# A fused attention and two gated MLPs: two more groups of heads of the first batch score in float32, after transposes on the matrix engine

## The chip, the cores and the metric

The kernel runs on one core of a Trainium2 chip. A core has five engines that run side by side, each through its own list of instructions in a fixed order: TensorE (PE, with its weight loads as PEld), VectorE (DVE), ScalarE (ACT), GpSimd (POOL) and SyncE (SP), which here issues nearly all DMAs. They meet through semaphores. The metric is the device time of one execution in microseconds (us), the median of several.

## The reference

```python
q_n, k_n = rmsnorm(q, g_q), rmsnorm(k, g_k)          # q, k, v: 4 x 12 x 448 x 64, float32
attn = softmax(q_n @ k_n.T / sqrt(64))
x = (attn @ v).transpose(0, 2, 1, 3).reshape(4, 448, 768)
h = relu(x @ w_in)                                   # w_in: 768 x 1024
x = (h * sigmoid(conv3(h))) @ w_out                  # w_out: 1024 x 768
out = (sigmoid(conv5(x)) * (x @ w_val)) @ w_out2     # both 768 x 768
```

The float64 weights come in as pairs of 32-bit words and are made into float32 on the chip.

## The kernel before, in words

A program does not issue its instructions where they are written. It records them, each with a due time that the numbers `S_*`, `W_*`, `C_*` and so on set, in a `Plan`. The planner (`order`, `forward`) then runs a small model of the engines and of the DMA queues over the record and writes each engine's list. Some operations may go to one of two engines (`copy`: DVE or ACT; `sub` and `vg`: DVE or POOL), and the planner picks.

The work is four batches. Batch b has 21 attention units: 3 groups (`r`) of 4 heads, each group with 6 units of 128 query rows and one for the 64 rows left over. The MLPs of batch b run on PE while the attention of batch b+1 is worked on. The attention of batch 0 has no MLP beside it: there the weights are loaded, made into float32 and split in two float16 halves (tiles `w`, `wi`, `wo`).

Products are exact enough only if an operand is kept as a float16 pair, high and low, with three matmuls for one, or as float32. A group's `prep` loads q (`qin`) and k (`kin`, two pairs of heads), sums squares, takes the inverse roots (`ssq`, `half`, `root`, DVE), and scales k on POOL (`kin<-kin,gb`, `kin<-kin,root`). Then there are two ways to `qa` and `ka`, the operands of the scores with the head dimension on the partitions:

- not `flat`: `split_q` and `norm_k`/`low_k` write float16 pairs (`tq`; `tk`, whose second buffer in batch 0 lies in `act`), and `turn_q`, `turn_k` transpose them with a DMA (`DMA_TRANSPOSE qa<-tq`, `ka<-tk`). `qk` then issues three matmuls for each head.
- `flat`: q goes as it is and k as scaled float32 through PE transposes into PSUM (7 for q, 4 for each k, banks `psm`), a copy takes them to `qa` and `ka`, and `qk` issues one float32 matmul for each head.

Before, only group 0 of batch 0 is `flat` (`FLAT_0`); groups 1 and 2 are not, nor is any group of the other batches. In all of batch 0 the probabilities `p` are float32 and transposed by PE (`psm<-ident,p`, copied to `pt`); in batches 1 to 3 they are float16 pairs and transposed by DMA (`pt<-p`). After the scores (`pss`, two PSUM buffers) DVE takes the row maximum (TENSOR_REDUCE `pss<-pss`, one a unit), ACT the exponential. The three `psm` banks serve the transposes, the left-over units and the MLPs.

Of the kernel before, what the change touches and what calls it, by code (L numbers as in the profile page):

```python
# [15 lines left out]
ALU = mybir.AluOpType  # L16
# [9 lines left out]
class Plan:  # L26
# [10 lines left out]
    HOP = {"tensor": 0.2, "vector": 0.13, "scalar": 0.16, "gpsimd": 0.09}  # L37
    WINDOW = 23.016
    AHEAD = 50.91
    URGENT = 0.595  # L40
    TICK = 10.24 / 3
    ENTRY = 3060.0

# [193 lines left out]
    def order(self):  # L237
# [42 lines left out]
    def forward(self, first, users, port, shape):  # L280
        ops, nops = self.ops, len(self.ops)
        left = [len(o[1]) for o in ops]
        ready = [o[2] for o in ops]
        ends = [None] * nops
        waiting = {e: [] for e in Plan.ENGINES}
        free = dict.fromkeys(Plan.ENGINES, 1.05)
        free["sync"] = 0.58

        def enter(i):
            for e in ops[i][0]:  # L290
                waiting[e].append(i)
# [12 lines left out]
        def begin(i, e):
            t = max(free[e], hold[e], ready[i])
            at = held[other_of[e]] if port[i][e] else 0.0
            return at + self.KEEP if at > t else t

        while len(result) < nops:
            best = None  # L310
            for e in Plan.ENGINES:
                if waiting[e]:
                    t = min(begin(i, e) for i in waiting[e])
                    if best is None or t < best[0]:
                        best = (t, e)
            t, e = best
            pick = None
            turn = self.SWITCH if e == "tensor" else 0.0
            for _, i in sorted(
                (first[i] + (turn if turn and shape[i] != now_shape else 0.0), i) for i in waiting[e] if begin(i, e) <= t  # L320
            ):
                ways, lean = ops[i][0], ops[i][3]
                mine = t + ways[e][0][0] + lean.get(e, 0.0)
                other = min(
                    (max(free[x], t, held[other_of[x]] if port[i][x] else 0.0) + ways[x][0][0] + lean.get(x, 0.0) for x in ways if x != e),
                    default=1e9,
                )
                if mine <= other + 0.4:
                    pick = i
                    break  # L330
            if pick is None:
                hold[e] = t + 0.05
                continue
            i = pick
            hold[e] = 0.0
            (busy, lag, data), method, a, k = ops[i][0][e]
            if port[i][e]:
                t = max(free[e], ready[i], held[other_of[e]])
            for x in ops[i][0]:
                waiting[x].remove(i)  # L340
            if e == "tensor":
                busy, lag = self.clocked(t, busy, lag, counts), 0.0
                if now_shape not in (None, shape[i]):
                    busy += 0.1
                now_shape = shape[i]
            if method.startswith("dma"):
                t = max(since + 0.03 if e == "scalar" else t, ready[i], hwdge)
                hwdge = t + 0.45
                behind = max(dma - t - 1.28, 0.0)
                dma = t + 1.28 + behind + data  # L350
                end = t + lag + (0.8 if method == "dma_start_transpose" else 1.0) * behind
                busy += (0.35 if method == "dma_start_transpose" else 0.08) * behind
                busy = max(free[e] - t, busy)
            else:
                end = t + busy + lag
            if e == "scalar":
                since = t
            free[e] = t + busy
            ends[i] = end + (0.0 if method.startswith("dma") else self.HOP[e]), busy
            if port[i][e]:  # L360
                held[e] = t + busy - (0.06 if e == "vector" else 0.09)
            result.append((t, len(result), i, e))
            for u in users[i]:
# [14 lines left out]
def kernel(  # L378
# [15 lines left out]
    real, nc = tc.nc, Plan()  # L394
    B, H, S, D = q.shape
# [68 lines left out]
    def vg(lean, method, *a):  # L464

        nc.add([(e, method, a, {}) for e in ("vector", "gpsimd")], vector=lean)

    def sub(lean, out, x, y):
        vg(lean, "tensor_tensor", out, x, y, ALU.subtract)
# [26 lines left out]
    EARLY_W = 20  # L496
    S_TQ = 2.041
    S_DQ = 0.439
    S_K0 = 0.983
    S_K1 = 9.27  # L500
    S_DK = 1.448
    S_LQ = 3.68
    S_LK = -0.859
    S_G = -2.706
    DT0 = 2.39
    DT_1 = 5.2
    DT_2 = 5.592
    DT_3 = 7.99
    LAG = 2
    A_EXP = 0.719  # L510
    C_GATE = 1.87
    C_MUL = 2.053
    C_HI = 2.928
    C_LO = 3.1
    V_HI = 0.658
    A_HI = 0.853
    A_LO = 1.304
    A_OUT = 0.172
    E_PTR = 0.83
    E_AV = 2.135  # L520
    X_LAG = 1.873
    MPE = 96.0
# [4 lines left out]
    D_IN = 3.4  # L527
    L_TAP = -0.036
    LATE = 1
    LATE_F = 10  # L530
    FOLD_Q = 0
    FOLD_K = 0
    SIGN_IN = 1
# [5 lines left out]
    D_Y = 2.44  # L539
    KLEAD = 3.639  # L540
    QLEAD = 3.701
    VLEAD = 5.253
    STAT = 0.406
    KD_ = 1.21
    QD_ = 1.199
    W_IN = -74.315
    W_IN_STEP = 1.774
    W_OUT = -15.789
    W_OUT_STEP = 2.498
    W_VAL = 28.433  # L550
    W_VAL_STEP = 2.317
    W_2 = 87.193
    W_2_STEP = 3.986
    RS_AT = -0.54
    RS_STEP = 1.052
    BIG_IN = 1
    BIG_OUT = 1
    BIG_VAL = 0
    BIG_2 = 0
    OUT = (0, 0, 4, 4)  # L560
    FLAT_0 = 0.942
    FLAT_1 = 0.0
    FLAT_2 = 0.0
    WIDE_0 = 1
    WIDE_1 = 1
    WIDE_2 = 1


    L_SQ = 1.689
    L_LOAD = 3.419  # L570
    L_WHI = 1.553
    L_WLO = 0.899
    L_ROOT = 0.317
    L_QHI = 0.565
    L_QLO = 0.924
    L_GAIN = 1.803
    L_NORM = 4.34
    L_KHI = 1.236
    L_KLO = 0.76
    L_PLO = 0.459  # L580
    L_VM = -0.01
    L_VHI = 0.976
    L_VLO = 1.029
    L_PHI = 2.301
    L_PT = 4.563
    L_XHI = -0.2
# [33 lines left out]
    def close_bank(ps):  # L620
        in_use.pop(next(i for i, x in enumerate(in_use) if x is ps))
# [186 lines left out]
    def prep(b, r, t0, tq, dq, tk_, dk, ahead):  # L808
# [90 lines left out]
        def gain_k(i):  # L899
            x3 = of_k(i)[2]  # L900
            vg(lean(L_GAIN, S_LK), "tensor_tensor", x3, x3, gain_b, ALU.mult)

        def norm_k(i):
# [3 lines left out]
            if flat:  # L907
                by = rr[:KR, cols(i)].rearrange("p (h c) -> p h c", h=2).unsqueeze(3).to_broadcast([KR, 2, KC, D])
                to = o.rearrange("p a c d -> p (a c d)").bitcast(F32).rearrange("p (c h d) -> p h c d", c=KC, h=2)
                vg(lean(L_NORM, S_LK), "tensor_tensor", to, x, by, ALU.mult)  # L910
                return
            vg(lean(L_NORM, S_LK), "tensor_tensor", x3, x3, rr[:KR, cols(i)].unsqueeze(2).to_broadcast([KR, 2 * KC, D]), ALU.mult)
            copy(lean(L_KHI, S_LK), hi, x)

        def low_k(i):
            j, x, x3, o, hi, lo = of_k(i)
            assert holds["kin", i] == holds["tk", i if b == 0 else 0] == (b, j)
            if not flat:
                sub(lean(L_KLO, S_LK), lo, x, hi)

# [103 lines left out]
    def smax(u):  # L1024
        u.m = mx[u.n % 4]
        u.rq = root[(u.b * NPR // 2 + u.r) % 3]
        i0, i1 = u.parts[0][3](0), u.parts[0][3](1)
        m = u.ps[:, 0, S : S + 2]
        nc.vector.tensor_reduce(m, u.ps[:, :, 0:S], AX.X, ALU.max, negate=True)
        nc.vector.tensor_tensor(u.m, m, u.rq[:, i0 : i1 + 1 : i1 - i0], ALU.mult)  # L1030
        if u.out:
            vg(L_ROOT, "tensor_scalar", u.m, u.m, math.log(SP), None, ALU.add)

# [212 lines left out]
    for u in units:  # L1246
        t, d = T(u.n), T(u.n + 1) - T(u.n)
# [31 lines left out]
    def mlp(b, before):  # L1279
# [14 lines left out]
        def w_in_tile(f):  # L1294
            st = {}
# [27 lines left out]
                nc.scalar.activation(st["a"], st["a"], AF.Tanh, scale=0.5 / SX)  # L1323

            def mul():
                nc.vector.scalar_tensor_tensor(st["h"], st["a"], 1.0, st["h"], ALU.add, ALU.mult)

            def hi():
                g16[f] = take()
# [1 line left out]

            def lo():
                g = pairv(g16[f])
                nc.vector.tensor_tensor(g[:, 1], st["h"], g[:, 0], ALU.subtract)
                close_bank(st["ps"])

            group(st, [step(kk) for kk in range(KD)], D_IN)
            t = clock[0]
# [224 lines left out]
```

## Time and profile before

| | |
|---|---|
| median of 3 runs | 670.3 us (667.63 to 670.92) |
| the profiled execution's own time | 669.94 us, span 668.0 us |
| mean granted TensorE clock, share of full | 0.957 |
| busy PE / DVE / ACT / POOL | 584.2 / 517.2 / 420.1 / 224.3 us |

An engine's busy time is what its instructions cover; a share over the whole span says little where stretches differ, so the rows below go by stretch. Line numbers of instructions all read L374: that is the planner's `emit`, so instructions are told apart by their tiles.

### The profile page before, as it was taken

What the parts mean: (1) busy time and instruction counts of PE and PEld (TensorE: products, weight loads), DVE (VectorE), ACT (ScalarE), POOL (GpSimd) and SP (SyncE); (2) the same over time, 40 slices, a digit from 0 to 9 for tenths busy, and PEclk for the clock granted to TensorE, in tenths of its full rate; (3) what the DMA queues carried; (4) which work ended last, traced back from release to release, by engine and by line L of the source; (5) the groups of instructions that cost most, each with busy time, mean ns of one, the idle gap of its engine ahead of it and who ended that gap; (6) DMA issues with size and microseconds to landing.
All of it is one profiled execution on the core that took longest, in us unless ns stands there. A gap on an engine that the chain in (4) does not pass through costs nothing.

```text
span 668.0 us, 12681 instructions
## 1 busy us (share of the span) xinstructions
PE 584.2 (87%) x4753; PEld 329.7 (49%) x4753; DVE 517.2 (77%) x1061; ACT 420.1 (63%) x736; POOL 224.3 (34%) x241
## 2 busy tenths in 40 slices
PE   3866988876969789769897999999899999999997
PEld 1554766443434444335454555555455556445554
DVE  5798989999899998989659685659889663687720
ACT  4887899689868676978647465448765452342211
POOL 2344535254245225557634144405542210000000
PEclk9996999878998979989999899999999999999999
DMA  8887679979679859967978448556734735000001
GB/s 199 168 201 156 142 168 203 231 136 207 135 151 227 213 117 184 204 147 153 186 164 162 81 94 158 123 120 109 141 75 69 140 80 126 19 0 1 1 24 60
DMA packets 254894, 88.12 MB, mean 132 GB/s; under 512 B 240955, under 2 KB 250737, under 8 KB 254833
## 3 DMA queue, kind: packets, MB, share of 16 engines
q1 hardware_dynamic: 254833, 87.31, 63.5%
q8 instruction: 37, 0.61, 0.4%
q14 instruction: 24, 0.20, 0.1%
HBM read 38.66 MB, written 5.51 MB: 66 GB/s over the span
## 4 chain that ended last, share of the span: by engine, by line
PE 37%; DVE 26%; DMA 13%; ACT 13%; issue 5%; POOL 3%; SPq 2%; ACTq 0%; POOLq 0%; DVEq 0%
PE psm L374 29%; DVE act L374 7%; DMA pt<-p 6%; ACT p L374 5%; PE psx L374 4%; DVE pss L374 4%; DVE scr L374 4%; PE pss L374 3%; DVE w L374 3%; SPq L374 2%; ACT act L374 2%; DVE psm L374 2%; DMA ka<-tk 2%; DMA w<-in_moe_w_val_dram 2%; DVE p L374 1%
## 5 line engine op out<-in xcount | busy, mean ns | idle before, releaser
L374 PE MATMUL psm<-act,wi 128*128 128x448 f16 x576 | 125.0, 367 | 9.7 <-DVE act L374 8.1
L374 PE MATMUL psm<-act,wo 128*128 128x448 f16 x576 | 120.5, 360 | 0.2 <-DVE act L374 0.2
L374 DVE TENSOR_REDUCE pss<-pss 128x2 f32<-128x896 f32 x84 | 90.6, 1091 | 17.1 <-PE pss L374 15.2
L374 PEld LDWEIGHTS <-pt 128*128 128x128 f16 (+1 forms) x1512 | 66.8, 104 | 63.8 <-DMA pt<-p 43.5
L374 PE MATMUL psm<-w,act 128*128 128x384 f16 (+1 forms) x576 | 90.7, 326 | 2.2 <-ACT osb L374 1.9
L374 PE MATMUL psm<-act,wv 128*128 128x448 f16 x432 | 90.4, 357 | 1.8 <-DVE act L374 1.8
L374 ACT ACTIVATE p<-pss,mx,root 128x448 f32<-128x448 f32 x112 | 76.1, 723 | 22.7 <-DVE mx L374 13.0
L374 ACT ACTIVATE act<-psm 128x448 f16<-128x448 f32 (+4 forms) x90 | 47.8, 540 | 64.0 <-DVE psm L374 36.2
L374 PEld LDWEIGHTS <-wi 128*128 128x128 f16 x576 | 56.3, 101 | 64.1 <-issue 23.1
L374 PE MATMUL pss<-ka,qa 64*128 64x448 f16 (+3 forms) x560 | 71.1, 389 | 14.6 <-ACT p L374 6.1
L374 PEld LDWEIGHTS <-wo 128*128 128x128 f16 x576 | 55.1, 99 | 52.3 <-issue 9.0
L374 PE MATMUL psx<-vv,pt 128*128 128x65 f16 (+1 forms) x1116 | 79.8, 206 | 0.0
L374 PEld LDWEIGHTS <-act 128*128 128x128 f16 (+1 forms) x576 | 49.1, 101 | 33.7 <-issue 5.1
L374 POOL TENSOR_TENSOR p<-p,p 128x896 f16<-128x896 f32 x27 | 51.3, 1903 | 42.4 <-ACT p L374 36.2
L374 DVE SCALAR_TENSOR_TENSOR act<-psm,cw,act 128x444 f32<-128x444 f32 (+3 forms) x96 | 63.9, 676 | 0.7
L374 PEld LDWEIGHTS <-wv 128*128 128x128 f16 x432 | 40.7, 99 | 39.8 <-issue 6.8
L374 PE MATMUL psx<-vm,pt 128*128 128x130 f16 (+1 forms) x186 | 27.8, 244 | 31.5 <-DMA pt<-p 20.7
L374 DVE SCALAR_TENSOR_TENSOR scr<-psm,cw,scr 128x447 f32<-128x447 f32 x64 | 43.1, 677 | 2.7 <-ACT scr L374 2.1
L374 DVE SCALAR_TENSOR_TENSOR w<-w 128x768 uint32<-128x768 uint32 (+1 forms) x56 | 44.3, 796 | 0.0
L374 ACT ACTIVATE p<-p 128x896 f16<-128x896 f32 x42 | 40.0, 952 | 3.4 <-DMA pt<-p 3.0
L374 ACT ACTIVATE osb<-psm 128x384 f32<-128x384 f32 x28 | 13.6, 490 | 45.2 <-PE psm L374 34.3
L374 PEld LDWEIGHTS <-qa 64*128 64x128 f16 (+1 forms) x528 | 20.7, 99 | 41.4 <-issue 27.1
(123 smaller groups left out, 925.5 us busy)
## 6 DMA issues: line engine op xcount, KB each, us to landing
w<-in_moe_w_in_dram SPq DMA_DIRECT2D x8, 768.0 KB, 5.4
w<-in_moe_w_out_dram SPq DMA_DIRECT2D x8, 768.0 KB, 5.8
kin<-in_k_dram SPq DMA_DIRECT2D x24, 224.0 KB, 3.7
qin<-in_q_dram SPq DMA_DIRECT2D x36, 128.0 KB, 3.6
act<-in_moe_w_out_dram SPq DMA_DIRECT2D x12, 384.0 KB, 3.8
w<-in_moe_w_val_dram SPq DMA_DIRECT2D x12, 384.0 KB, 3.9
out_dram<-osb SPq DMA_DIRECT2D x24, 192.0 KB, 2.1
vst<-in_v_dram SPq DMA_DIRECT2D x18, 224.0 KB, 3.5
```

The source lines that it names most:

```text
L374: getattr(getattr(nc, e), method)(*a, **k)
```

## The change

`FLAT_1` and `FLAT_2` go from 0 to 1: groups 1 and 2 of batch 0 take the `flat` way too. The planner's model of DMA issues charges the issuing queue differently, and some 40 due times and leanings get new values. Two new switches, `MUL` and `LEAVE_IN`, are off and add no instruction.

```diff
-                end = t + lag + (0.8 if method == "dma_start_transpose" else 1.0) * behind
-                busy += (0.35 if method == "dma_start_transpose" else 0.08) * behind
+                end = t + lag + behind
+                busy += (0.15 if method == "dma_start" else 1.0 if data > 1.6 else 0.3) * behind
...
-    FLAT_0 = 0.942
-    FLAT_1 = 0.0
-    FLAT_2 = 0.0
+    FLAT_0 = 0.908
+    FLAT_1 = 1
+    FLAT_2 = 1
...
-    URGENT = 0.595
+    URGENT = 0.616
...
-    W_VAL = 28.433
-    W_VAL_STEP = 2.317
+    W_VAL = 26.105
+    W_VAL_STEP = 2.348
...
+    MUL = 0.0
+    LEAVE_IN = (0, 0, 0, 0)
```

Some 40 numbers more change in the same tables. What they and the planner make of it is seen in the lists of instructions, at three places.

On DVE, between the last row maximum of group 0 and the first of group 1 (`root_106` is group 1's inverse root, `kin`/`tk` and `kin`/`act` are the low halves of its two k). The end of that piece, before: 12 rows, the maximum itself comes 7 rows later.

```order
L374 TENSOR_REDUCE ssq_104<-act 128x14
L374 TENSOR_SCALAR rs_110<-psm_121 128x2
L374 RECIPROCAL rs_110<-rs_110 128x2
L374 TENSOR_TENSOR scr_95<-psm_121,rs_110 128x128
L374 TENSOR_TENSOR tk_86<-kin_83,tk_86 112x2x4x64
L374 TENSOR_SCALAR w_65<-w_65 128x768
L374 TENSOR_TENSOR act<-kin_84,act 112x2x4x64
L374 TENSOR_SCALAR rs_109<-psx_118 128x6
L374 TENSOR_TENSOR act<-psm_120,act 128x64
L374 RECIPROCAL rs_109<-rs_109 128x6
L374 CAST act<-psm_120 128x64
L374 TENSOR_TENSOR scr_96<-psx_118,rs_109 128x384
```

The changed program has, for the end of that piece, the maximum as the eighth row:

```order
L374 SCALAR_TENSOR_TENSOR root_106<-half_108,root_106 128x30
L374 SCALAR_TENSOR_TENSOR half_108<-root_106 128x30
L374 TENSOR_TENSOR half_108<-half_108,ssq_104 128x30
L374 SCALAR_TENSOR_TENSOR root_106<-half_108,root_106 128x30
L374 TENSOR_REDUCE ssq_104<-act 128x14
L374 CAST act<-psm_120 128x384
L374 TENSOR_TENSOR act<-psm_120,act 128x384
L374 TENSOR_REDUCE pss_117<-pss_117 128x2
L374 TENSOR_SCALAR rs_110<-psm_121 128x2
L374 TENSOR_REDUCE pss_116<-pss_116 128x2
```

Before, 25 rows stand between the two maxima, two of them k's low halves; now 14, and no split of k.

On PE, at the first scores of group 1 (`qa_69`). Before, they come straight behind batch 0's attention products and a transpose of the convolution weights (`act 128x24`); each score has a weight load of its own row.

```order
L374 MATMUL psx_118<-vm_75,pt_92 128x130
L374 MATMUL psx_118<-vv_71,pt_92 128x65 x6
L374 MATMUL psm_120<-ident,scr_95 128x128
L374 MATMUL psm_120<-ident,act 128x24
L374 LDWEIGHTS qa_69
L374 MATMUL pss_117<-ka_66,qa_69 128x448
L374 LDWEIGHTS qa_69
L374 MATMUL pss_117<-ka_66,qa_69 128x448
```

In the changed program the transposes of k (`ident,tk`, and `ident,act` for the second k) stand between the products, and a unit has four score matmuls:

```order
L374 MATMUL psm_120<-ident,tk_86 128x112 x4
L374 MATMUL psx_118<-vm_75,pt_92 128x130
L374 MATMUL psx_118<-vv_71,pt_92 128x65 x3
L374 MATMUL psm_120<-ident,scr_94 128x128 x3
L374 MATMUL pss_117<-ka_66,qa_69 128x448 x2
L374 MATMUL pss_116<-ka_66,qa_69 128x448 x2
L374 MATMUL psm_121<-vv_71,pt_93 64x65
L374 MATMUL psm_120<-ident,p_0_88 128x128 x3
L374 MATMUL psx_118<-vv_71,pt_92 128x65 x3
L374 MATMUL psm_120<-ident,act 128x112 x4
```

On SP, the queue of DMAs from group 1's first k on. Before:

```order
L374 DMA_TRANSPOSE ka_66<-tk_86 128x8x112
L374 DMA kin_83<-in_k_dram 112x8x64
L374 DMA kin_84<-in_k_dram 112x8x64
L374 DMA_TRANSPOSE ka_67<-act 128x8x112
L374 DMA w_65<-in_moe_w_in_dram 128x6x256
L374 DMA vv_71<-in_v_dram 128x7x64
L374 DMA w_65<-in_moe_w_in_dram 128x6x256 x2
L374 DMA_TRANSPOSE ka_66<-tk_86 128x8x112
L374 DMA kin_83<-in_k_dram 112x8x64
L374 DMA w_65<-in_moe_w_out_dram 128x1536
```

In the changed program the same loads stand without the transposes of groups 1 and 2; the first DMA transpose of the program is the one of batch 1 in the last row:

```order
L374 DMA kin_83<-in_k_dram 112x8x64
L374 DMA kin_84<-in_k_dram 112x8x64
L374 DMA vv_70<-in_v_dram 128x7x64
L374 DMA vv_71<-in_v_dram 128x7x64
L374 DMA w_65<-in_moe_w_in_dram 128x6x256 x2
L374 DMA qin_85<-in_q_dram 128x4x64
L374 DMA qin_85<-in_q_dram 64x2x64 x2
L374 DMA qin_85<-in_q_dram 128x4x64 x2
L374 DMA kin_83<-in_k_dram 112x8x64
L374 DMA kin_84<-in_k_dram 112x8x64
L374 DMA_TRANSPOSE qa_69<-tq_87 128x14x128
```

Over the whole program the changed lists have 6 DMA transposes fewer (2 of q, 4 of k), 30 PE transposes more (14 of q, 16 of k), 8 copies from PSUM more on ACT, 1 score matmul for each 3 in two groups, on DVE 3 float16 casts and 1 low half of q and 3 low halves of k fewer, on POOL 1 low half of q fewer, and 3 of the 8 low halves of `wi` that POOL did are now on DVE.

## Rows read from the trace of the kernel before

**Rows 1.** The page: busy time of each engine, share of the span.
```profile
PE 584.2 (87%) x4753; PEld 329.7 (49%) x4753; DVE 517.2 (77%) x1061; ACT 420.1 (63%) x736; POOL 224.3 (34%) x241
```

**Rows 2.** Busy time by stretch; columns: PE, PEld, DVE, ACT, POOL, clock, DMA share.
```profile
16.50:40.70 24.20, 20.95 (x140) 14.35 (x136) 20.82 (x46) 20.79 (x38) 9.96 (x7) 1.00 0.76 171
40.70:52.90 12.20, 6.73 (x71) 5.36 (x71) 11.26 (x26) 7.28 (x15) 6.04 (x5) 0.77 1.03 219
52.90:75.00 22.10, 18.07 (x147) 13.09 (x143) 19.00 (x44) 19.76 (x35) 9.89 (x9) 0.82 0.54 127
75.00:111.00 36.00, 31.96 (x297) 24.27 (x297) 32.93 (x73) 33.24 (x59) 16.86 (x30) 1.00 0.80 168
111.00:255.00 144.00, 116.36 (x979) 59.85 (x978) 136.22 (x276) 112.46 (x201) 56.76 (x55) 0.89 0.86 181
255.00:405.00 150.00, 132.72 (x1120) 72.01 (x1118) 118.35 (x243) 98.51 (x173) 73.49 (x70) 0.95 0.77 153
405.00:556.00 151.00, 144.77 (x1347) 79.83 (x1346) 112.26 (x231) 91.09 (x152) 47.60 (x43) 1.00 0.61 114
556.00:668.00 112.00, 106.90 (x655) 58.04 (x652) 56.95 (x92) 29.48 (x56) 0.00 (x0) 1.00 0.09 27
```

**Rows 3.** Timeline of DVE (start, length): score reduces and the k split.
```profile
39.62 1.08 DVE L374 TENSOR_REDUCE pss<-pss 128x2 f32<-128x896 f32 x1
...
45.71 1.89 DVE L374 TENSOR_TENSOR tk<-kin,tk 112x512 f16<-112x512 f32 x1 [0.71 <-ACT tk L374]
...
47.99 0.68 DVE L374 TENSOR_TENSOR act<-kin,act 112x512 f16<-112x512 f32 x1
...
52.90 1.08 DVE L374 TENSOR_REDUCE pss<-pss 128x2 f32<-128x896 f32 x1
...
73.94 1.10 DVE L374 TENSOR_REDUCE pss<-pss 128x2 f32<-128x896 f32 x1
...
80.40 2.10 DVE L374 TENSOR_REDUCE pss<-pss 128x2 f32<-128x896 f32 x2 [0.38 <-PE pss L374]
...
84.84 1.10 DVE L374 TENSOR_REDUCE pss<-pss 128x2 f32<-128x896 f32 x1
...
93.39 2.10 DVE L374 TENSOR_REDUCE pss<-pss 128x2 f32<-128x896 f32 x2 [0.34 <-PE pss L374]
```

**Rows 4.** Timeline of POOL.
```profile
43.41 2.05 POOL L374 TENSOR_TENSOR kin<-kin,root 112x512 f32<-112x512 f32 x2 [2.15 <-DVE root L374]
45.42 1.64 POOL L374 TENSOR_TENSOR wi<-w,wi 128x768 f16<-128x768 f32 x1
...
72.37 2.05 POOL L374 TENSOR_TENSOR kin<-kin,root 112x512 f32<-112x512 f32 x2 [1.23 <-DVE mx L374]
```

**Rows 5.** Timeline of PE: transposes, float32 scores, float16 scores.
```profile
12.32 1.01 PE L374 MATMUL psm<-ident,tk 112*128 112x112 f32 x4 [2.66 <-DVE tk L374]
13.96 3.36 PE L374 MATMUL pss<-ka,qa 64*128 64x448 f32 x8 [0.63 <-ACT ka L374]
...
30.95 0.98 PE L374 MATMUL pss<-ka,qa 64*64 64x448 f32 x8
...
36.66 1.02 PE L374 MATMUL pss<-ka,qa 64*128 64x448 f32 x4
37.73 1.27 PE L374 MATMUL psm<-ident,act 128*128 128x128 f32 x7
...
51.31 2.43 PE L374 MATMUL pss<-ka,qa 64*128 64x448 f16 x12 [1.26 <-DMA ka<-tk]
...
64.01 0.77 PE L374 MATMUL pss<-ka,qa 64*64 64x448 f16 x12
...
73.16 0.74 PE L374 MATMUL pss<-ka,qa 64*128 64x448 f16 x6
...
111.12 2.07 PE L374 MATMUL psm<-act,wi 128*128 128x448 f16 x10
```

**Rows 6.** Chain that ended last, in order of time: start, length, what.
```profile
74.85 1.17 POOL tk L374
76.04 3.46 DMA ka<-tk
79.50 6.17 DMA ka<-act
```

**Rows 7.** Groups by line and operation, the whole span.
```profile
L374 DVE SCALAR_TENSOR_TENSOR w<-w 128x768 uint32<-128x768 uint32 (+1 forms) x56 | 44.3, 796 | 0.0
...
L374 ACT ACTIVATE tk<-kin 112x512 f16<-112x512 f32 (+1 forms) x38 | 24.1, 634 | 5.7 <-DMA ka<-tk 3.4 <-DVE ssq L374 1.2 <-DMA kin<-in_k_dram 0.7
...
L374 DVE TENSOR_TENSOR act<-psm,act 128x448 f16<-128x448 f32 (+2 forms) x44 | 24.2, 554 | 4.2 <-ACT act L374 4.0
...
L374 ACT ACTIVATE tq<-qin 128x896 f32<-128x896 f32 (+1 forms) x17 | 16.2, 955 | 2.2 <-DMA qin<-in_q_dram 1.4 <-DVE ssq L374 0.7
...
L374 DVE TENSOR_SCALAR w<-w 128x768 uint32<-128x768 uint32 (+1 forms) x23 | 12.1, 525 | 1.1 <-ACT w L374 0.9
...
L374 DVE CAST tq<-qin 128x896 f16<-128x896 f32 x3 | 2.2, 748 | 0.0
...
L374 DVE TENSOR_TENSOR tq<-qin,tq 128x896 f16<-128x896 f32 x2 | 2.2, 1080 | 0.0
...
L374 ACT ACTIVATE ka<-psm 128x448 f32<-128x448 f32 x2 | 1.1, 540 | 1.0 <-PE psm L374 1.0
...
L374 DVE TENSOR_TENSOR wi<-w,wi 128x768 f16<-128x768 f32 x1 | 1.0, 958 | 0.3 <-ACT wi L374 0.3
```

**Rows 8.** Waits in 120 to 200 us: who waited for whom, total, times, longest.
```profile
PEld L374 <- DMA pt<-p: 16.0, 7, 5.4
...
PE psx L374 <- DMA pt<-p: 8.1, 4, 5.0
```

More of the change, by code (lines that the diff above doesn't have):

```diff
@@ L498 @@
     S_DQ = 0.439
-    S_K0 = 0.983
-    S_K1 = 9.27
-    S_DK = 1.448
+    S_K0 = 0.442
+    S_K1 = 10.999
+    S_DK = 1.13
     S_LQ = 3.68
-    S_LK = -0.859
-    S_G = -2.706
+    S_LK = -0.847
+    S_G = -2.904
     DT0 = 2.39
@@ L510 @@
     A_EXP = 0.719
-    C_GATE = 1.87
+    C_GATE = 1.957
     C_MUL = 2.053
-    C_HI = 2.928
+    C_HI = 2.839
     C_LO = 3.1
[L515 to L519, printed above, removed]
+    V_HI = 0.539
+    A_HI = 0.812
+    A_LO = 1.313
+    A_OUT = 0.204
+    E_PTR = 0.82
     E_AV = 2.135
@@ L529 @@
     LATE = 1
-    LATE_F = 10
+    LATE_F = 11
     FOLD_Q = 0
@@ L541 @@
     QLEAD = 3.701
-    VLEAD = 5.253
-    STAT = 0.406
-    KD_ = 1.21
+    VLEAD = 5.408
+    STAT = 0.347
+    KD_ = 0.835
     QD_ = 1.199
     W_IN = -74.315
-    W_IN_STEP = 1.774
+    W_IN_STEP = 1.534
     W_OUT = -15.789
-    W_OUT_STEP = 2.498
-    W_VAL = 28.433
-    W_VAL_STEP = 2.317
+    W_OUT_STEP = 2.513
+    W_VAL = 26.105
+    W_VAL_STEP = 2.348
     W_2 = 87.193
@@ L554 @@
     RS_AT = -0.54
-    RS_STEP = 1.052
+    RS_STEP = 1.09
     BIG_IN = 1
@@ L569 @@
     L_SQ = 1.689
-    L_LOAD = 3.419
+    L_LOAD = 3.339
     L_WHI = 1.553
     L_WLO = 0.899
-    L_ROOT = 0.317
-    L_QHI = 0.565
+    L_ROOT = 0.301
+    L_QHI = 0.519
     L_QLO = 0.924
-    L_GAIN = 1.803
-    L_NORM = 4.34
+    L_GAIN = 1.744
+    L_NORM = 4.365
     L_KHI = 1.236
     L_KLO = 0.76
-    L_PLO = 0.459
-    L_VM = -0.01
+    L_GLO = 0.494
+    L_MUL = 1.0
+    MUL = 0.0
+    LEAVE_IN = (0, 0, 0, 0)
+    L_PLO = 0.462
+    L_VM = -0.011
     L_VHI = 0.976
-    L_VLO = 1.029
+    L_VLO = 1.023
     L_PHI = 2.301
@@ L1027, in smax @@
         i0, i1 = u.parts[0][3](0), u.parts[0][3](1)
-        m = u.ps[:, 0, S : S + 2]
+        m = u.m if MUL else u.ps[:, 0, S : S + 2]
         nc.vector.tensor_reduce(m, u.ps[:, :, 0:S], AX.X, ALU.max, negate=True)
-        nc.vector.tensor_tensor(u.m, m, u.rq[:, i0 : i1 + 1 : i1 - i0], ALU.mult)
+        by = u.rq[:, i0 : i1 + 1 : i1 - i0]
+        if MUL:
+            vg(L_MUL, "tensor_tensor", u.m, m, by, ALU.mult)
+        else:
+            nc.vector.tensor_tensor(u.m, m, by, ALU.mult)
         if u.out:
@@ L1325, in mul @@
             def mul():
-                nc.vector.scalar_tensor_tensor(st["h"], st["a"], 1.0, st["h"], ALU.add, ALU.mult)
+                to = st["a"] if LEAVE_IN[b] else st["h"]
+                nc.vector.scalar_tensor_tensor(to, st["a"], 1.0, st["h"], ALU.add, ALU.mult)
+                st["h"] = to
+                if LEAVE_IN[b]:
+                    close_bank(st["ps"])
             def hi():
@@ L1333, in lo @@
                 g = pairv(g16[f])
-                nc.vector.tensor_tensor(g[:, 1], st["h"], g[:, 0], ALU.subtract)
-                close_bank(st["ps"])
+                if LEAVE_IN[b]:
+                    sub(L_GLO, g[:, 1], st["h"], g[:, 0])
+                else:
+                    nc.vector.tensor_tensor(g[:, 1], st["h"], g[:, 0], ALU.subtract)
+                    close_bank(st["ps"])
             group(st, [step(kk) for kk in range(KD)], D_IN)
```

## The prediction

> **What bounds the kernel now.** The page comes first: PE is busy 87% of the span, DVE 77% [rows 1], and neither share says where a change bites. The table by stretch does [rows 2]. From 556 us on there is only the last MLP, PE 106.90 of 112 us. From 255 to 556 PE is busy 92% (277.5 of 301 us) and DVE 77%: PE is the bound. From 111 to 255 us, where batch 0's MLPs and batch 1's attention run, DVE is busy 136.22 of 144 us, 94.6%, and PE 81%: DVE is the bound. Ahead of that lies batch 0's attention, 16.5 to 111 us, and this is where the change works. Its groups have the same work and not the same time. Group 0, already in float32, runs at 86% on PE, DVE and ACT alike. The 12.2 us behind it, 40.7 to 52.9, are odd: PE is busy 6.73 us, ACT 7.28, and the granted clock is 0.77, for DVE alone is at work. From 40.7 to 111, 70.3 us, the sums are DVE 63.19, ACT 60.28 and PE 56.76, so PE idles 13.5 us.
>
> The row maxima on DVE show where attention stands still [rows 3]. Inside a group they come some 3.5 us apart (52.90 to 73.94: six steps). Between the last of group 0 (39.62) and the first of group 1 (52.90) lie 13.28 us, and between group 1 (73.94) and group 2 (80.40) 6.46. What lies there is the way of k. At the first boundary POOL scales k until 45.46, ACT rounds it, DVE takes the low half from 45.71 for 1.89 us [rows 3, 4], the DMA transposes, and PE's scores can begin at 51.31, released by that DMA [rows 5]. At the second, the scaling ends at 74.42, the chain goes over the low half on POOL (until 76.02) to the DMA of the first k (3.46 us), and then to that of the second k, 6.17 us more, to 85.67 [rows 4, 6]. Both DMA stretches are on the chain that ended last.
>
> **The change part by part.**
>
> *The way of k and q, first boundary.* The low half, the rounding and the DMA go; four PE transposes and a copy come. Group 0 shows this way at work [rows 5]: transposes from 12.32, scores from 13.96, 1.64 us with the copy between. Put behind the scaling that ends at 45.46, with 0.1 us of hand-over, the scores begin at 47.2 in place of 51.31. A unit's float32 scores take 1.02 us, so the maximum comes at 48.3 where 52.90 stands: 4.6 us. The lists set the other bound: 14 rows of DVE stand between the two maxima in place of 25. They are the maximum itself (1.08 us), a sum of squares (about 1.1 at the same size), three passes over weights (2 x 0.80 + 0.53 = 2.1), two halves of x (0.55 each) and small ones (some 0.8), 6.2 us in all against 13.28: up to 7 us [rows 7].
>
> *Second boundary.* Scaled by 74.42, scores from 76.2, maximum at 77.3 for 80.40: 3.1 us. The second k no longer waits for a DMA until 85.67; the maxima at 84.84 and 93.39 are 8.55 us apart [rows 3], but PE had other products queued there, so I count nothing for it and keep up to 3 us as the upper side.
>
> *PE pays.* Twelve units of 128 rows change from 0.74 to 1.02 us, two left-over units from 0.77 to 0.98 [rows 5]: 3.8 us. Transposes: seven of 128x128 took 1.27 us where PE was warm, four of k 1.01 us at the start; per group 1.3 + 2 x 1.0 = 3.3, two groups 6.6. If a k transpose costs what a q one does there (0.18), it is 2 x (1.3 + 1.45) = 5.5. So 9.3 to 10.4 us more PE work, in a stretch that idles 13.5. It is hidden there as long as the transposes stand in those gaps; if that cover were gone, it would cost all of it. Some comes back, since the twelve scores at 51.31 took 2.43 us at the low clock where two units take 1.48 at the full one. The Trainium skill, page "VectorE: DVE Perf Modes", section "The three transpose paths", gives 390 ns for a 128x128 transpose on TensorE and 1309 ns for the DMA's. Thirty at 390 ns would be 11.7 us and the PE bill 15.5, above the idle time; the rows give 5.5 to 6.6, and I go by them.
>
> *ACT.* Eight copies of about 0.54 us come (4.3 us), one rounding of q (0.95) and four of k (0.63) go (3.5): nothing, within 1 us [rows 7].
>
> *DVE and POOL.* DVE loses three casts of q over the whole program (0.75 each), a low half of q (1.1) and three of k (0.68 undisturbed, 1.89 once) and gets three low halves of `wi` at 0.96 [rows 3, 7]: 2.2 + 1.1 + 3.2 - 2.9 = 3.6 us less. The 1.89 us is the same form as the 0.68 us behind it; while it ran, POOL was in `wi<-w,wi` until 47.06 [rows 4]. POOL loses work of that sort too, so DVE may be held up less; I take 1 us of that and leave the rest.
>
> *SP.* Six DMA transposes less. Loads behind them go out earlier; the weights they bring are not what DVE waits for in batch 0, so nothing.
>
> *The planner's new charge for DMA issues, and the new numbers.* They move rows in all four batches. The trace of before can't price it. Bounds: PE's weight loads waited 16.0 us and PE 8.1 us for `pt<-p` between 120 and 200 us [rows 8]; a better order could save some 9 of these 24, a worse one cost as much. I take nothing.
>
> *The sum.* The boundaries give 4.6 + 3.1 = 7.7. DVE must still do its work: 63.19 less about 2 in that stretch, at the 94.6% it holds in the next one, is 64.7 us for 70.3, so 5.6 are to be had and I take 5.5. In 111 to 255 DVE is the bound, and the other 1.5 us of its 3.6 come off directly. From 255 us on the work is the same and starts 7 us earlier. So 669.94 - 7 = 663 for the profiled execution, whose time is within 0.4 of the median 670.3; I predict 663.
>
> **The rivals.**
>
> *The gain is eaten by PE.* For: PE needs 56.76 + 10 of 70.3 us already, with ACT at 60 and DVE at 61; no stretch so far holds three engines above 90%. Group 0, with this way, ran at 86%, and PE's 66.8 at 95% are 70.3 again: the first stage is as long as before. Only DVE's 0 to 3 us later remain: 667 to 670, say 669. Against: the gaps that the transposes fill are there, and the clock was low in them. The 390 ns of the Trainium skill ("VectorE: DVE Perf Modes", the section named above) would make this the likeliest; the rows, where 128x128 transposes follow each other in 0.18 us, do not agree.
>
> *Slower: the three `psm` banks.* Each of the eight fills must be copied by ACT before its bank serves again, and PE's list is in order: a transpose that waits for a bank holds the products behind it. If each waits for a pair of exponentials and two copies of `pt` (some 2.4 us) it is 19 us, of which the 3.5 us of PE idle left hide little: 15.5 - 7 = 8.5 slower, 678. It decides from some 1.3 us per fill (8 x 1.3 = 10.5 = 3.5 + 7). For: 0.86 of ACT is busy. Against: group 0's transposes of the second k stand between products with no such wait.
>
> *Much faster, by the order of DMA issues.* If a third of those 24 us of waits for `pt<-p` goes, 8 us come on top: 655. For: such waits stand in all stages to 500 us. Against: it hangs on a model's constants.
>
> *The `flat` way changes nothing because planner and pools move the stall elsewhere* falls with the first rival.
>
> **How the numbers follow.** About 0.5% (3.3 us) is what a measurement of this kernel tells from no change. The forecast, 658 to 667, has 0.45; the PE rival 0.22; the slower one 0.15; the much faster one 0.18. Faster by over 0.5% (below 666.9): 0.45 + 0.18 = 0.63. Within: 0.22. Slower: 0.15. The forecast's own range is 658 to 667. The range for eight in ten must reach into both outer cases: 651 leaves out the far third of the much faster one, 674 most of the slower one: 651 to 674.
>
> **What would show it.** Right: the maxima of groups 0 and 1 come 6 to 9 us apart; no DMA of k on the chain before 100 us; the first `wi` matmul, at 111.12 before [rows 5], comes at 105 to 106; DVE stays above 93% to about 250 us. Wrong: that matmul at 110 or later with PE above 93% in the stretch (PE rival), or with PE waiting for ACT's `ka`, `qa` and `pt` copies (banks); or the first stage as forecast and the gain gone by 255 us, which would say that DVE wasn't the bound of the second stage; or a gain that grows behind 255 us, which would be the order of issues.

## The result, and the profile after

The change makes the kernel slower: 675.5 us (median of 14 runs, 672.5 to 681.2) against 668.8 us for the kernel before, measured beside it (14 runs). The ratio is 1.0091, with a 95% interval of 1.0064 to 1.0117. Forecast were 663 us and faster. The profiled execution of the changed kernel took 680.07 us (span 678.3), at the upper end of its runs.

The page's busy times beside [rows 1]:

```profile
PE 593.9 (88%) x4751; PEld 335.9 (50%) x4751; DVE 512.6 (76%) x1057; ACT 423.1 (62%) x739; POOL 218.0 (32%) x238
```

DVE has 4.6 us less to do, as forecast (3.6), PE 9.7 more. The table by stretch, beside [rows 2] (columns: span of the stretch, then busy us of PE, PEld, DVE, ACT and POOL, the granted clock, DMA share, GB/s):

```profile
40.70:52.90 12.20, 10.03 (x89) 7.43 (x89) 8.79 (x22) 9.86 (x18) 7.92 (x6) 1.00 0.75 169
52.90:75.00 22.10, 20.10 (x118) 15.61 (x117) 15.32 (x41) 15.31 (x29) 4.19 (x4) 0.82 0.32 93
75.00:111.00 36.00, 31.64 (x220) 22.24 (x218) 31.18 (x58) 29.79 (x53) 15.68 (x22) 0.88 0.58 138
111.00:255.00 144.00, 113.67 (x1031) 61.18 (x1030) 135.19 (x269) 113.77 (x198) 54.04 (x56) 0.94 0.87 178
```

The first boundary got what it was to get: from 40.7 to 52.9 us PE is busy 10.03 us, where it was 6.73. But from 52.9 to 111 us the granted clock is 0.82 and 0.88 while PE is at work, and DVE, which was to be the limit, is busy only 69% of 52.9 to 75 us (15.32 of 22.1 us). The row maxima on DVE, beside [rows 3], show where attention now stands:

```profile
37.61 1.10 DVE L374 TENSOR_REDUCE pss<-pss 128x2 f32<-128x896 f32 x1 [0.35 <-PE pss L374]
47.38 1.09 DVE L374 TENSOR_REDUCE pss<-pss 128x2 f32<-128x896 f32 x1
...
54.93 1.10 DVE L374 TENSOR_REDUCE pss<-pss 128x2 f32<-128x896 f32 x1 [0.56 <-PE pss L374]
68.95 1.09 DVE L374 TENSOR_REDUCE pss<-pss 128x2 f32<-128x896 f32 x1
...
77.27 1.10 DVE L374 TENSOR_REDUCE pss<-pss 128x2 f32<-128x896 f32 x1 [3.14 <-PE pss L374]
80.27 1.09 DVE L374 TENSOR_REDUCE pss<-pss 128x2 f32<-128x896 f32 x1
89.89 1.09 DVE L374 TENSOR_REDUCE pss<-pss 128x2 f32<-128x896 f32 x1
```

Groups 0 and 1 are 9.8 us apart (13.3 before), groups 1 and 2 are 3.0 (6.5 before). Two new long gaps between maxima stand elsewhere: 14.0 us from 54.93 to 68.95, and 9.6 from 80.27 to 89.89. The windows of 5 us, and then the two gaps as a whole:

```profile
55.00:60.00 5.00, 4.18 (x27) 2.64 (x26) 4.05 (x10) 4.20 (x10) 1.57 (x2) 1.00 0.10 19
60.00:65.00 5.00, 5.00 (x27) 4.97 (x27) 3.16 (x12) 2.09 (x5) 0.00 (x0) 0.50 0.77 248
65.00:70.00 5.00, 5.00 (x33) 4.18 (x32) 3.26 (x11) 3.12 (x6) 0.00 (x0) 0.81 0.14 48
70.00:75.00 5.00, 3.86 (x25) 2.92 (x25) 3.61 (x8) 3.79 (x7) 2.61 (x2) 0.87 0.42 96
75.00:80.00 5.00, 5.00 (x26) 2.45 (x24) 2.73 (x5) 4.13 (x8) 0.94 (x2) 0.79 0.40 91
105.00:110.00 5.00, 5.00 (x23) 4.10 (x24) 3.60 (x2) 3.84 (x7) 3.37 (x3) 0.50 0.74 145
...
54.93:68.95 14.02, 13.20 (x75) 10.86 (x76) 9.50 (x31) 8.81 (x17) 1.57 (x2) 0.76 0.36 112
80.27:89.89 9.62, 9.05 (x83) 6.65 (x81) 9.59 (x19) 8.20 (x17) 5.02 (x14) 1.00 0.52 120
```

PE is busy the whole time at the half clock (0.50, 1.2 GHz), from 60 to 67, 74 to 77 and 104 to 111 us. Before, the half clock lay at 47 to 61 us, where PE was busy 5.89 of 14 us. In the first gap PE sets the pace at the low clock, and DVE is busy 9.50 of 14.02 us. The second is no stall: at the full clock DVE is busy 9.59 of its 9.62 us and PE 9.05, with other rows. PE's timeline around the fall, beside [rows 5]:

```profile
58.99 0.96 PE L374 MATMUL pss<-ka,qa 64*64 64x448 f32 x2 [0.82 <-ACT p L374]
...
64.60 1.38 PE L374 MATMUL psx<-vv,pt 128*128 128x65 f32 x6
...
67.85 1.02 PE L374 MATMUL pss<-ka,qa 64*128 64x448 f32 x4
...
121.42 0.73 PE L374 MATMUL psm<-act,wi 128*128 128x448 f16 x3
```

Ahead of the fall PE waited 0.82 us. A float32 matmul leaves two records in the trace (96 for the 48 float32 score matmuls of the changed kernel): `x4` is one unit's two score matmuls, not the four that I gave a unit above, and `x6` three products of A·V. These three take 1.38 us here and 0.78 at the full clock. The next scores stand behind 7.8 us of such work, from 60.05 to 67.85. The first `wi` matmul comes at 121.42 us, 10.3 later than before [rows 5].

For what follows I add up what the half clock takes from PE: in windows of 1 us, PE's busy time times one less the granted clock. Up to 111 us this **lost PE time** is 2.9 us in the kernel before and 8.3 in the changed one. Over the whole span it is nearly the same, 20.9 and 21.2 us: the change moved it from 111 to 255 us, where DVE is the bound (12.6 before, 7.3 after), into the first stage.

### The profile page after: what moved, and what is told of

Its sections match the earlier page's. It is cut to its first block, busy times and chain, and to the rows that moved or that the text cites. A ratio compares the mean times of both kernels' runs of the same rounds, so it can differ in the third digit from the quotient of the medians.

```text
span 678.3 us, 12672 instructions
## 1 busy us (share of the span) xinstructions
PE 593.9 (88%) x4751; PEld 335.9 (50%) x4751; DVE 512.6 (76%) x1057; ACT 423.1 (62%) x739; POOL 218.0 (32%) x238
## 4 chain that ended last, share of the span: by engine, by line
PE 39%; DVE 26%; DMA 16%; ACT 8%; issue 6%; POOL 2%; SPq 2%; ACTq 0%; DVEq 0%; POOLq 0%
PE psm L374 29%; DMA pt<-p 11%; DVE act L374 7%; PE psx L374 6%; DVE pss L374 4%; DVE scr L374 4%; PE pss L374 4%; ACT p L374 4%; DVE w L374 3%; SPq L374 2%; DVE psm L374 2%; ACT act L374 2%; DMA w<-in_moe_w_val_dram 2%; DMA qin<-in_q_dram 1%; DVE p L374 1%
## 5 line engine op out<-in xcount | busy, mean ns | idle before, releaser
L374 PE MATMUL psm<-act,wv 128*128 128x448 f16 x432 | 93.7, 362 | 4.3 <-DVE act L374 4.2
L374 PE MATMUL psm<-w,act 128*128 128x384 f16 (+1 forms) x576 | 92.2, 327 | 0.4 <-DVE act L374 0.4
L374 PE MATMUL psx<-vv,pt 128*128 128x65 f16 (+1 forms) x1116 | 85.6, 206 | 1.0 <-ACT pt L374 1.0
L374 PE MATMUL pss<-ka,qa 64*128 64x448 f16 (+3 forms) x528 | 75.9, 417 | 12.0 <-DVE p L374 5.2
L374 PE MATMUL psx<-vm,pt 128*128 128x130 f16 (+1 forms) x186 | 26.2, 235 | 26.2 <-DMA pt<-p 24.5
L374 POOL TENSOR_TENSOR kin<-kin,gb 112x512 f32<-112x512 f32 x22 | 29.3, 1332 | 35.3 <-ACT tk L374 15.6
```

The source lines that it names most:

```text
L374: getattr(getattr(nc, e), method)(*a, **k)
```

## The experiments

Sixteen runs. Theory F: the float32 way itself costs, by PE work and half clock. Theory N: the new due times lose. Theory M: the new charge for DMA issues loses. Each timed run was measured in five rounds beside the kernel before.

| kernel | median us | ratio to before, interval | lost PE time to 111 us | first `wi` matmul |
|---|---|---|---|---|
| e1 float32 groups alone | 686.3 | 1.0235 (1.0189 to 1.0281) | 15.3 | 128.1 |
| e2 all but float32 groups | 668.5 | 0.9975 (0.9942 to 1.0009) | 0.0 | 103.8 |
| e3 changed, old charge | 675.0 | 1.0063 (1.0033 to 1.0092) | 4.9 | 114.8 |
| e4 new charge alone | 675.1 | 1.0083 (1.0053 to 1.0112) | 7.1 | 116.9 |
| e5 new numbers alone | 671.3 | 1.0032 (1.0001 to 1.0064) | 11.5 | 120.8 |
| e7 e1, gaps filled | 681.2 | 1.0153 (1.0102 to 1.0205) | 3.4 | 115.9 |
| e8 changed, gaps filled | 668.3 | 0.9986 (0.9951 to 1.0020) | 0.0 | 115.3 |
| e9 e2, more PE work | 670.6 | 1.0017 (0.9981 to 1.0052) | 0.0 | 107.4 |
| e10 changed, filled elsewhere | 673.0 | 1.0068 (1.0031 to 1.0105) | 7.9 | 121.9 |
| e11 before, filled | 674.7 | 1.0080 (1.0041 to 1.0118) | 3.0 | 116.6 |
| e12 e8, later gaps filled too | 678.7 | 1.0151 (1.0100 to 1.0202) | 3.3 | 117.0 |
| e13 group 1 alone float32 | 674.2 | 1.0054 (1.0013 to 1.0096) | 1.6 | 110.6 |

The last two columns are from the one profiled execution of each.

### Which part of the change

e1 is the kernel before with

```diff
-    FLAT_1 = 0.0
-    FLAT_2 = 0.0
+    FLAT_1 = 1
+    FLAT_2 = 1
```

> The kernel before with FLAT_1 and FLAT_2 at 1 and nothing else of the change. Theory F (the float32 way itself costs: PE gets some 10 us more work in the first stage, and part of the stage falls to the half clock, 1.2 GHz, while PE is fully busy): 674 to 680 us, first wi matmul at 117 us or later, windows of 5 us with PE at 4.9 or more at a granted clock near 0.50 between 55 and 110 us. Theory N (the float32 way gives the forecast 5 to 7 us, the new due times lose more): 661 to 666 us, first wi matmul at 105 to 107. Theory M (the new charge for DMA issues loses it, behind 111 us): 661 to 666 us as well.

e2 is the changed kernel with `FLAT_1 = FLAT_2 = 0.0`:

> The changed kernel with FLAT_1 and FLAT_2 back at 0: the new charge and the new numbers stay. Theory F: 666 to 671 us, first wi matmul at 109 to 113 us, and no window of 5 us at half clock with PE fully busy before 111 us. Theory N or M: 674 to 680 us; under N with the first wi matmul late already (115 us or more), under M with the loss behind 111 us.

e3 is the changed kernel with the old lines for `end` and `busy` in the planner:

> The changed kernel with the old charge for DMA issues in the planner's model: the float32 groups and the new numbers stay. Theory F: 674 to 679 us, as the changed kernel. Theory N: the same. Theory M: 664 to 669 us, with the waits for pt<-p on the chain back near 5 or 6% of the span from 11%.

e4 is the kernel before with the new ones:

> The kernel before with the new charge for DMA issues alone. Theory F and theory N: 667 to 672 us, as before. Theory M: 674 us or more, with the loss behind 111 us.

e5 is the changed kernel with the old charge and without the float32 groups:

> The changed kernel without the float32 groups and with the old charge for DMA issues: the new due times alone. If the new numbers are worth 1% as the pair of the charge alone (675.1) and the charge with the numbers (668.5) suggests: 662 to 667 us. If charge and numbers only fit each other: 667 to 673 us. The theories on the float32 way say nothing of it beyond this: no half clock with PE busy before 111 us, or a later first wi matmul by half of what there is.

The float32 groups cost 2.3% by the old numbers (e1) and 1.2% by the new (e2 against the changed kernel): theory F holds in this, though e1 lies 6 us above its range and the `wi` matmul of e2 5 us ahead of the expected one. N and M fall as the cause of the loss: e2 isn't slower, and e3 without the new charge is (its waits for `pt<-p` are 7% of the chain, 11% in the changed kernel). e4 missed what F said of it, 667 to 672: the charge alone is slower too, with 7.1 us of lost PE time and float16 groups. e5 came in the second of its ranges, with 11.5 us lost and the `wi` matmul 17 us behind e2's, without any float32 group more than before. So the half clock is no property of the float32 way; it strikes float16 orders too. Nor does the lost time up to 111 us price a kernel of another order: e5 loses 11.5 us there and is 0.3% slower than before, e4 loses 7.1 and is 0.8% slower. e1 by windows of 5 us:

```profile
30.00:35.00 5.00, 3.47 (x25) 1.92 (x25) 4.56 (x13) 4.06 (x7) 3.02 (x3) 0.99 0.58 168
35.00:40.00 5.00, 5.00 (x17) 2.88 (x13) 3.35 (x9) 2.74 (x6) 0.00 (x0) 0.50 0.52 158
40.00:45.00 5.00, 5.00 (x19) 3.47 (x17) 2.95 (x8) 2.83 (x6) 0.00 (x0) 0.50 0.25 69
45.00:50.00 5.00, 4.95 (x24) 4.55 (x24) 1.39 (x4) 3.58 (x6) 2.05 (x2) 0.50 0.72 205
50.00:55.00 5.00, 5.00 (x44) 4.66 (x44) 2.57 (x5) 3.32 (x6) 1.40 (x1) 0.50 0.36 72
```

Behind one gap of 1.47 us PE works 20 us at half speed almost without a pause, and DVE and ACT starve beside it. e2 shows something else. Its first boundary is as short as that of the changed kernel, with float16 and the DMA:

```profile
45.28 1.31 PE L374 MATMUL pss<-ka,qa 64*128 64x448 f16 x12 [0.83 <-DMA ka<-tk]
...
47.63 2.08 DVE L374 TENSOR_REDUCE pss<-pss 128x2 f32<-128x896 f32 x2
```

Its last maximum of group 0 is at 38.80, so the boundary takes 8.8 us, where the kernel before takes 13.28 [rows 3] and the changed one 9.8. The DMA of the first k is through 6.0 us earlier than in [rows 5]. The last column of the table has to be read with care between lists: in e2's the first `wi` matmul (103.81) stands ahead of batch 1's first scores (104.66), in the changed one behind three units of them (in e8 at 104.66, 111.74 and 113.01, then `wi` at 115.30).

### Is it the clock

The theories left within F are the half clock, the amount of PE work and the order of rows. Filling tells the first from the others: where the trace shows PE idle ahead of a fall, transposes of the identity matrix go into its list, into a bank that the next real transposes overwrite. For e8:

```diff
+FILL = {185: (6, 188), 237: (8, 239), 313: (11, 317), 366: (14, 371)}
...
+            if e == "tensor":
+                count, into = FILL.get(n, (0, 0))
+                for _ in range(count):
+                    nc.tensor.transpose(self.ops[pe[into]][0][e][2][0], self.fill, self.fill)
+                n += 1
             getattr(getattr(nc, e), method)(*a, **k)
```

> The kernel with the float32 groups alone, and 51 extra transposes of the identity matrix on PE, put into the six places where its trace shows PE idle for 0.58 to 2.59 us in the first stage just ahead of a fall of the granted clock; each writes a PSUM bank that the next real transposes overwrite. Only waiting time is filled, no other work changes. If the half clock under full PE work is what costs (it had some 33 us of it up to 117 us, worth half of that): the clock stays up, time falls by 8 to 16 us from 686 to 670 to 678 us, first wi matmul from 128 to 112 to 120 us. If the cost is the amount of PE work or the order of rows: 686 us or up to 6 us more.

> The changed kernel with 39 extra transposes of the identity matrix in the four places of the first stage where its trace shows PE idle for 0.8 to 2.2 us (58.2, 72.6, 89.8 and 101.9 us). If the half clock costs (17 us of it with PE busy, worth 8 or 9): the first wi matmul comes at 112 to 116 in place of 121.4 us and the time is 666 to 671 us. If the work or the order costs: 675 us or up to 5 us more.

e8's windows and two of its rows, to be laid beside those of the changed kernel above:

```profile
55.00:60.00 5.00, 4.99 (x33) 3.24 (x33) 3.89 (x15) 3.61 (x7) 0.77 (x2) 1.00 0.27 83
60.00:65.00 5.00, 5.00 (x43) 4.23 (x42) 4.49 (x17) 4.28 (x7) 0.00 (x0) 1.00 0.71 231
```

```profile
57.04 0.88 PE L383 MATMUL psm<-ident 128*128 128x128 f32 x6
...
63.67 1.02 PE L385 MATMUL pss<-ka,qa 64*128 64x448 f32 x4
```

Thirty-nine useless transposes (5.1 us of PE) keep the clock at 1.00 up to 111 us, bring the scores that stood at 67.85 to 63.67, and take 1.05% (7 us) off the time; time and `wi` matmul both lie in the ranges of the clock. e7 gained 0.8%, less than expected (681.2 us for 670 to 678), with one episode left. Its remaining 1.5% over before is not lost PE time of the first stage (3.4 us against 2.9 in the profiles): by the old numbers something else costs too, order or work, which these runs don't part.

e10 puts as many transposes into three places where PE had no gap:

```diff
+FILL = {278: (13, 278), 295: (13, 295), 330: (13, 330)}
```

> A control for the filled gaps: the changed kernel with the same number of extra transposes of the identity matrix, 39, in three places of the first stage where its trace shows PE busy without a gap (82.3, 85.8 and 95.2 us, 13 each). If filling worked through the clock: the half clock stays (6 us or more of PE time lost to it up to 111 us) and the time is 675 to 680 us. If any shift of PE's work would have done it: 671 us or less.

The lost time stays at 7.9 us, though at other places (falls at 20, 51 and 105 us), the first `wi` matmul at 121.9. At 673.0 us it lies below the expected range and above e8, whose interval it does not touch. Of the 1.05% some 0.8 are between these two, which differ in where the same transposes stand: most of the gain is the clock's.

e9 adds the work without the clock: e2 with three transposes ahead of each half of p's transposes in groups 1 and 2 (`FILL = {152: (3, 152), 162: (3, 162), ...}`, 28 places).

> The changed kernel without the float32 groups (668.5 us, full clock all through the first stage), with three extra transposes of the identity matrix ahead of each half of the transposes of p in groups 1 and 2: 84 in all, some 9 us of PE work at 0.11 us each, as much as the float32 way adds. Nothing waits for them but PE's own list. If the amount of PE work is what costs: 674 to 679 us, first wi matmul 6 to 10 us later than 103.8. If the work is hidden in PE's idle time and the clock (or the order) is what costs: 667 to 671 us.

PE's busy time grows by 8.1 us (585.3 for 577.2), the time by 0.4% by the two ratios, which the intervals can't tell from nothing; the `wi` matmul comes 3.6 us later than in e2, not the 6 to 10 of the first theory. PE's idle time hides most of such work at the full clock.

### The same program, several times

e13 takes group 2 back to float16 (`FLAT_2 = 0.0`). Its twelve times fall in two clusters, four at 667.3 to 669.7 us and eight at 673.6 to 677.0; its median, 674.2, lies in none of the ranges expected.

> The changed kernel with group 2 back on float16 (FLAT_2 at 0), group 1 float32. If each group costs by its share of the way: 671 to 673 us, between the changed kernel without float32 groups (668.5) and with both (675.5). If the cost is the half clock, it follows the clock of the first stage and not the number of groups: 668 us plus what the trace shows as PE time lost at half clock up to 111 us, with a spread of 2 us. If the float32 way is worth something by itself and only the clock spoils it: below 667 us where no half clock shows.

> A second profiled execution of the kernel with group 1 alone in float32, whose twelve times fall in two clusters (667 to 670, and 673.6 to 677; the first profile, 669.3 us, lost 1.6 us of PE time to the half clock up to 111 us, 3.3 up to 130). If time follows the clock: an execution of 673.6 us or more shows 5 us or more lost up to 130 us and the first wi matmul 3 us or more later than 110.55; one of 667 to 670 us shows about 3 us. If it doesn't: the two don't go together.

> A third execution of the same program, with the same expectation: 673.6 us or more with 5 us or more of PE time lost to the half clock up to 130 us, or 667 to 670 us with about 3 us; no relation if the clock isn't the cause.

> A second profiled execution of the changed kernel (times 672.5 to 681.2; the first, 680.07 us, lost 8.3 us of PE time to the half clock up to 111 us, with the first wi matmul at 121.4). If time follows the clock: an execution of 673 to 676 us shows 2 to 6 us less lost and the first wi matmul earlier by about as much; one near 680 us shows 8 us again. If order or work is all: the first stage is the same to 1 us in both whatever the time.

> A second profiled execution of the changed kernel with the four gaps filled (times 664.6 to 673.9; the first, 666.07 us, lost nothing up to 130 us and 7.2 us from 111 to 255). If filling holds the clock by itself: 0 to 2 us lost up to 111 us again and the first wi matmul at 115 to 117, at any time in its spread. If the first was a lucky execution: 5 us or more lost up to 111 us and a time above 670 us.

The first profile of this program (669.3 us) and its second (676.5 us) run alike up to 52 us: the same scores start 0.06 us apart, behind the same waits of PE (1.06, 0.58 and 0.62 us in the one, 1.07, 0.58 and 0.62 in the other). Then they take 1.02 us in the first and 1.68 in the second:

```profile
52.53 1.02 PE L374 MATMUL pss<-ka,qa 64*128 64x448 f32 x4
...
52.47 1.68 PE L374 MATMUL pss<-ka,qa 64*128 64x448 f32 x4
```

Further on, the first profile and then the second in the same windows:

```profile
65.00:70.00 5.00, 4.36 (x27) 2.78 (x26) 3.91 (x15) 4.11 (x8) 0.00 (x0) 1.00 0.01 3
70.00:75.00 5.00, 4.67 (x60) 4.29 (x60) 4.42 (x10) 3.94 (x9) 3.07 (x3) 1.00 0.07 14
75.00:80.00 5.00, 4.50 (x40) 3.50 (x39) 5.00 (x7) 3.50 (x8) 2.95 (x8) 1.00 0.96 184
```

```profile
65.00:70.00 5.00, 4.55 (x19) 2.78 (x20) 3.71 (x13) 3.71 (x6) 0.00 (x0) 0.64 0.00 0
70.00:75.00 5.00, 4.42 (x8) 1.38 (x6) 2.11 (x9) 2.44 (x4) 0.00 (x0) 0.50 0.02 3
75.00:80.00 5.00, 5.00 (x25) 5.00 (x25) 2.99 (x6) 2.21 (x4) 2.05 (x2) 0.50 0.00 0
```

The list is the same; the clock differs first, and the times after it. Lost PE time up to 130 us is 3.3, 13.3 and 9.9 us in the three profiles, the first `wi` matmul comes at 110.6, 119.9 and 116.8, and the times are 669.3, 676.5 and 677.5 us, as the clock theory expected of both repeats. The first profile is from another chip than the other two; but among the twelve times, all from the first chip, the four short ones have a mean granted clock of 0.960 to 0.964, and the eight long ones 0.948 to 0.959. That is the plainest evidence, for nothing was edited.

The changed kernel a second time took 675.0 us with the same 8.4 us lost up to 111, where 2 to 6 us less were expected, and the `wi` matmul at 118.8. So its spread of 5 us is not the lost time of the first stage. Of the 5.1 us, 2.6 are there by the `wi` matmul and 4.5 by the first row maximum of batch 2, the 43rd of the trace (270.12 and 265.62); what makes them stays open. The filled one a second time lost 1.7 us and had its `wi` matmul at 115.5, at 669.5 us, as expected if filling works: it holds most of the clock, not all of it each time.

### Two that failed

e11 fills the kernel before (`FILL = {141: (38, 163), 153: (30, 159)}`):

> The kernel before with 68 extra transposes of the identity matrix in the two gaps of PE ahead of and inside its half clock at 47 to 60 us (38 ahead of the first scores of group 1, 30 ahead of the third). PE was nearly idle there, 6.0 us busy of 14, so the half clock cost at most 3 us. Clock theory: full clock at 47 to 60 us, time 666 to 670 us, within 0.5% of before. If the clock counted whatever PE does: 662 us or less. If extra work on PE costs: 672 us or more.

I put the transposes one row too late:

```profile
50.52 0.30 PE L386 MATMUL psm<-ident,act 24*128 24x24 f32 x1 [3.76 <-DVE act L386]
50.75 7.19 PE L384 MATMUL psm<-ident 128*128 128x128 f32 x38
57.87 1.31 PE L386 MATMUL pss<-ka,qa 64*128 64x448 f16 x12
```

They stand behind a small transpose that itself waits 3.76 us, so the gap stayed, the clock fell in it, and 38 transposes took 7.19 us, most of them at half speed (0.19 each; in e8, at the full clock, 0.13). The scores came 6.6 us later than in [rows 5], and the kernel is 0.8% slower, in the third of its ranges. It says nothing about the clock in the kernel before; it shows what PE work costs when it isn't covered.

e12 adds five more gaps, up to 299 us, to e8. A part of its output isn't the reference's: I take it that one of these groups of transposes writes a bank whose product hadn't all been read. The amount of work is the same.

> The changed kernel with the four gaps of the first stage filled as before (668.3 us) and five more gaps, which stand ahead of the half-clock episodes that were left (133.3, 177.8, 222.1, 296.0 and 299.3 us): 91 more transposes of the identity matrix. Those episodes cost PE 5.8 + 3.7 + 5.6 + 5.7 us of busy time at half speed, 10 us lost in all. If the half clock costs only where PE sets the pace: the first three lie where DVE is the bound and give nothing, the last gives up to 3 us: 665 to 668 us. If it costs everywhere: 658 to 663 us. If the extra transposes delay what waits behind them: 669 us or more.

It is 1.6% slower than e8, in the third of its ranges. The lost time from 111 to 405 us is 9.8 us, 10.0 in e8: the gaps moved and the episodes with them. What the half clock costs behind 111 us stays open.

## Why the prediction was wrong

**The way of k.** The boundaries shortened, by 3.5 us of 4.6 and by 3.5 where 3.1 was forecast; no DMA of k is on the chain in batch 0. But that is not the float32 way's merit, and that the second forecast came near is luck: with the same numbers and float16, e2's boundaries take 8.8 and 2.4 us. I took the 13.28 us for the length of the float16 way. It was the length in one order of rows, in which k's scaling and low half came late.

**PE pays.** This step failed. The size was right: busy time less lost time over the whole program is 572.7 us after (593.9 - 21.2) and 563.3 before (584.2 - 20.9), 9.4 us more. Such work is also largely hidden at the full clock, as e9 shows. What the sum lacks is the clock. I priced the work at the full clock, took the low clock for a mark of PE's idle stretches and wrote only that its loss would come back. I did not ask where it would lie once PE had work in the low stretch. It then lay on work: PE was busy 5.00 of 5 us at 0.50 from 60 to 65 us, 8.3 us were lost up to 111 us, and 7 us of time come back when the gaps are filled. A term for it was missing, and with it a rival.

**DVE, ACT, POOL.** DVE's 3.6 us less measured 4.6, POOL fell by 6.3, ACT rose by 3.0 where I had nothing, within 1. None of it decided.

**The sum.** The first stage was to be 5.5 us shorter and was 10.3 longer in the profiled execution, which ended 10.1 us later: there the loss passed to the end whole. It need not: e5 has its `wi` matmul 9.6 us later than before and its profiled execution ends 0.4 us earlier. From 111 to 255 us DVE was busy 93.9% (135.19 of 144 us), as forecast. A second step failed beside the clock: the sum let DVE hold 94.6% in the first stage too. From 40.7 to 111 us it held 79% in the changed kernel (55.29 of 70.3 us) and 84% in e8 at the full clock (59.37). So the forecast 7 us are not there even without the clock's loss: e8 ends at 0.9986 of before, at most 0.5% faster by its interval, and e2 at 0.9975. The first maxima of batch 2 are one row in every trace; before, the changed kernel, e2 and e8:

```profile
260.60 2.09 DVE L374 TENSOR_REDUCE pss<-pss 128x2 f32<-128x896 f32 x2
270.12 2.09 DVE L374 TENSOR_REDUCE pss<-pss 128x2 f32<-128x896 f32 x2
260.08 2.09 DVE L374 TENSOR_REDUCE pss<-pss 128x2 f32<-128x896 f32 x2
259.99 2.09 DVE L385 TENSOR_REDUCE pss<-pss 128x2 f32<-128x896 f32 x2
```

e2 and e8 are there within 0.6 us of before, though e2's first `wi` matmul comes 7.3 us earlier than before and e8's 4.2 later. So the sign that I chose, this matmul at 105 to 106 us, did not measure the gain: e2 has it at 103.8 and gains nothing that its interval tells. e8 still has 10.9 us between the 11th and 12th maximum, where PE is busy all the time, and 10.3 between the 15th and 16th, where DVE is busy 9.68 us and PE 9.26. What eats the rest, this order or the work itself, is open; no run undid it.

**The rivals.** "Eaten by PE" was nearest: the `wi` matmul behind 110 us, PE busy 94% in both long gaps (13.20 of 14.02 and 9.05 of 9.62 us). It had 669 us, for it too knew only one clock; e8, at the full one, has 668.3. The banks have nothing to do with it, the longest wait of PE in the first gap is the 0.82 us. The order of issues is no gain: the new charge alone loses 0.8%; beside the new numbers it goes from 1.0063 to 1.0091 with the float32 groups and from 1.0032 to 0.9975 without, neither of them outside the intervals. The last rival, that planner and pools move the stall elsewhere, I let fall with the first; the first of the new gaps is of that kind, but at the half clock.

## What to carry to other kernels

When a change puts work into a stretch where the matrix engine stood idle at the half clock, price that work at both levels, and ask which gap will stand ahead of it; a sum at the full clock alone leaves out the dearer case. A long gap between two marks is a stall only if the engine behind them waits, so read its busy time first, and compare a mark between two kernels only where both lists have it at the same place. Before giving a short boundary to the new way of computing, look whether the old way in another order would have it too: running the change without its main part costs one run. Where one program's times fall in two clusters, profile it twice and lay the clock's rows side by side.

## What the runs showed of the hardware

The clock fell to the half behind gaps of 0.82 us (the changed kernel, 58.2 to 59.0) and 1.47 us (e1), though PE had been busy 4.18 and 3.47 of the 5 us before. In e2 gaps of 1.90, 1.65 and 1.48 us (ending at 50.6, 63.4 and 83.9 us) brought no fall. It then stayed low with PE busy by its records without a pause for 3 to 20 us. The Trainium skill, page "TensorE: Matmul & The Clock Gate", Part 1, has the half rate as the state of an idle PE and the full one as that of a busy PE; these rows do not let the one be told from the other by busy time. And one list of instructions got 3.3, 13.3 and 9.9 us of lost time up to 130 us in three executions; behind the same 0.62 us of waiting the clock fell in the second and not in the first. So behind which gap it falls can't be read off the program.
